# Order of the first pairs' work in a sliding-window attention with a feed-forward layer: mask products, sums and zero fills moved between queues

## The chip, the cores and the metric

The kernel runs on one core of a Trainium2 chip. Its time is the device time of one execution in microseconds (us); several executions are timed and the median is taken. A core has five engines that run side by side, each with its own queue of instructions in order: TensorE (PE, matrix products into PSUM), VectorE (DVE), ScalarE (ACT), GpSimd (POOL) and SyncE (SP, which here only issues transfers). They wait for each other by semaphores. [...]

## The reference

```python
# q, k, v: (8 batches, 8 heads, 576 tokens, 64)
scores = q @ k.T / sqrt(64)              # per batch and head
scores = where(|i - j| <= 32, scores, -1e9)
attn = softmax(scores)
x = attn @ v                             # joined over heads: (4608, 512)
h = x @ w_in                             # (512, 2048)
g = maximum(0.01 * h, h)
out = g @ w_out                          # (2048, 512)
```

## The kernel before

Matrix products are in bf16, sums in fp32 PSUM. Heads go in pairs, so a batch has four pairs (128 rows of head dimension), and batches 0 and 1 (`BY_DMA = 2`) are done in halves of 288 tokens: attention step i of these is batch i // 8, half (i // 4) % 2, pair i % 4 (`where`). From step 16 (`OLD`) on, batches 2 to 7 are done in another form, in groups of four blocks of 64 tokens (`score_blocks`, `product_blocks`), with two buffers `sets[0]` and `sets[1]` used in turn.

For batch 0 one attention step is spread over the engines like this:

- `load_qk` (SP) brings the queries and keys of a pair in fp32; `load_cast_v` (POOL queue) brings the values of one head at a time as bf16 onto the diagonal blocks of `vbd`, whose other blocks have to be zero. Two such loads belong to a pair.
- `cast_qk` casts queries (`qb`) and keys (`kb`) to bf16; the engine of each can be chosen, and POOL is the default. L270 is its line for VectorE and POOL, L268 for ScalarE.
- `transposes` (a generator: each `next` does the queries or the keys of one pair) transposes on TensorE (L308); ScalarE copies the result out (L316 queries, L322 keys).
- `score(i)`: ten small matmuls (L409), the exponential on ScalarE (`e`, L421), and the product with the mask (`prob`, L423) on POOL, for step 0 on VectorE. In the changed file these two are two lines further up.
- `sums(i)`: two matmuls with a matrix of ones (L447) and VectorE's reciprocal (L452).
- `product(i)`: five matmuls of values and probabilities (L463); `scaled(i)`: VectorE multiplies by the reciprocal (L477) and writes `xT`, the input of the feed-forward layer.

`s` and `x`, the PSUM tiles of sums and products, have one buffer each, so a sum waits until the reciprocal before it is done, and a product until the scaling before it is done. The score tile `ps` has one for these steps too. The reciprocals `r` have three.

The order within each engine is that of the program text (`manual_schedule`), with no planner for this part. Feed-forward work for a half of 288 tokens is 16 hidden tiles (`h_tile`, L501 and L512), each of four chunks, one for each pair. The first four tiles of the first half go chunk by chunk (`h_first`), so that the chunk of a pair can start when that pair is scaled. `warm_up` (L602) and `keep_busy` (L610) are matmuls whose results nobody uses. `load_w_in` and `load_w_out` bring the weights in four parts each, on POOL's queue (L661, L665).

Batch 1 is prepared meanwhile. `kbd[1]` (keys on diagonal blocks) and `vbd[1]` (values) lie in `sets[1]` and each have four blocks of 128 x 1152, one for each pair, which are filled with zeros: six of the eight on POOL in the loop of the hidden tiles (L750), two on VectorE (L771). `clear_half(i, p, a, eng)` fills the unused half of the queries' place `qz[i]` for two pairs, which batches from 2 on read; for `qz[1]` two of the four calls come at the start on ScalarE (L221) and two in `second_pair` on VectorE (L226). `second_pair(p)` transposes batch 1's pairs and starts casts and loads. In the later part `step()` does one attention step, started from a plan of the feed-forward matmuls (`spend`).

Of the kernel before, what the change touches and what calls it, by code (L numbers as in the profile page):

```python
# [10 lines left out]
BF16 = mybir.dt.bfloat16  # L11
AF = mybir.ActivationFunctionType
# [4 lines left out]
def kernel(  # L17
# [15 lines left out]
    nc = tc.nc  # L33
# [8 lines left out]
    NB = S // 64  # L42
    HALF = S // 2
# [6 lines left out]
    const = ctx.enter_context(tc.tile_pool(name="const", bufs=1))  # L50
# [94 lines left out]

    ident_f = sets[1].bitcast(FP32)[:, N_SET // 2 - 320:N_SET // 2 - 192]
    make_identity(nc, ident_f)
    for p in range(2):
        nc.vector.memset(vbd[0][:, p], 0.0)
    ident = const.tile([128, 128], BF16)  # L150
# [3 lines left out]
    nc.vector.memset(ones_bd, 0.0)  # L154
    nc.vector.memset(ones_bd[0:64, 0:64], 1.0)
    nc.vector.memset(ones_bd[64:128, 64:128], 1.0)


    zero = const.tile([128, 1], BF16)
    nc.vector.memset(zero, 0.0)  # L160

    mask = [const.tile([128, 2, 2, EVEN], BF16, name=f"mask{i}") for i in range(2)]
    nc.vector.memset(mask[0][:, 1, :, 0:16], 0.0)
# [52 lines left out]
    def clear_half(i, p, a, eng):  # L216

        r = slice(64 * (1 - a), 64 * (1 - a) + 64)
        to = qz[i][r, p:p + 2, :, a].rearrange("p n g s -> p (n g) s")
        if eng is nc.scalar:  # L220
            eng.activation(  # L221
                out=to, in_=zero[r].to_broadcast([64, 2 * S]).rearrange("p (g s) -> p g s", s=192),
                func=AF.Copy,
            )
        else:
            eng.memset(to, 0.0)  # L226
# [35 lines left out]
    def cast_qk(b, p, q_eng=nc.gpsimd, k_eng=nc.gpsimd):  # L262
        for eng, src, dst in ((q_eng, qf, qb), (k_eng, kf, kb)):
            if eng is None:
                continue
            to, tok = dst[:, p], src[b, p].rearrange("p a (c d) -> p c a d", d=D)
            if eng is nc.scalar:
                eng.activation(out=to, in_=tok, func=AF.Copy)  # L268
            else:
                eng.tensor_copy(out=to, in_=tok)  # L270
# [127 lines left out]
    def score(i, masked_by=nc.gpsimd):  # L398
        if i >= OLD:
            return score_blocks(i)  # L400
        b, hf, p = where(i)
        by_c = qT[b][:, p].rearrange("p (c i) -> p c i", c=2)
        if b == 0:

            for a, n_, m in ((0, 0, 0), (1, 1, 0), (0, 0, 1), (1, 1, 1), (0, 0, 2),
                             (0, 1, 0), (1, 0, 0), (0, 1, 1), (1, 0, 1), (1, 0, 2)):
                blk, i0, n = WIN[hf][n_][m]
                r = slice(64 * a, 64 * a + 64)
                nc.tensor.matmul(  # L409
                    ps_v[r, n_, :, i0:i0 + n], first_keys[p][r, 64 * blk:64 * blk + 64],  # L410
                    by_c[r, :, hf * EVEN + i0:hf * EVEN + i0 + n], start=True, stop=True,
                )
        else:
            for n_, blocks in enumerate(WIN[hf]):
                for blk, i0, n in blocks:
                    nc.tensor.matmul(
                        ps_v[:, n_, :, i0:i0 + n], kbd[b % 2][:, p, blk],
                        by_c[:, :, hf * EVEN + i0:hf * EVEN + i0 + n], start=True, stop=True,
                    )
        e = attn.tile([128, 2 * HALF], BF16, name="e")  # L420
        nc.scalar.activation(out=e, in_=ps[:, P0:P0 + 2 * HALF], func=AF.Exp, scale=scale)  # L421
        pr = prob[:, i % NPROB]
        masked_by.tensor_mul(  # L423
            pr.rearrange("p n c i -> p (n c i)"), e, mask[hf].rearrange("p n c i -> p (n c i)"),
        )
        probs[i] = [pr, None, None]
# [123 lines left out]
    def h_first(g):  # L550

        hs = [mmps.tile([128, 512], FP32, name="mm", tag="mm") for _ in range(4)]
        yield hs[0]
        for c in range(DMC):
            for f in range(4):
                h_mms(g, f, hs[f], (c,))
            if c == DMC - 1:
                for f in range(4):
                    h_out(g, f, hs[f])
            yield  # L560
# [45 lines left out]
    def keep_busy(t, lo, n):  # L606


        for _ in range(n):
            nc.tensor.matmul(  # L610
                t[:, lo:lo + 224], ones_bd, mask[0].rearrange("p n c i -> p (n c i)")[:, 0:224], start=False, stop=False,
                skip_group_check=True,
            )
# [16 lines left out]
    def step():  # L630
        i = state["done"]
        if JOINED - 1 <= i < OLD - 1:
            join(i + 1)
        if i < NC - 2:
            score(i + 2)
        weighted(i)
        place_keys()
        place_queries()
        for b, p in qk_due.get(i, ()):
            cast_qk(b, p)  # L640
            transpose_dma(b, p)
        if i == OLD - 2:
            for a in range(2):
                clear_half(0, 2, a, nc.gpsimd)
        if i == OLD + NPAIR:
            clear_k(1)
            set_ones(1, 0, nc.gpsimd)
            set_ones(1, 2, nc.gpsimd)
        for b, p in v_due.get(i, ()):
            cast_vw(b, p)  # L650
        for part in v_next.get(i, ()):
            load_v_pairs(*part)
        for b, p in qk_next.get(i, ()):
            load_qk(b, p)
        state["done"] += 1
# [4 lines left out]
    def load_w_in(f0, f1):  # L660
        nc.gpsimd.dma_start(out=w_in_bf[:, :, f0:f1], in_=w_in_r[:, :, f0:f1])  # L661

    def load_w_out(i):
        c = slice(4 * i, 4 * i + 4)
        nc.gpsimd.dma_start(out=w_out_bf[:, c, :], in_=w_out_r[:, c, :])  # L665

    first = transposes(0)

    for a in range(2):
        clear_half(1, 0, a, nc.scalar)  # L670
    cast_qk(0, 0, nc.vector, nc.vector)
    make_mask(0)
    load_cast_v(0, 0)
# [8 lines left out]
    next(first)  # L682
    next(first)
    load_cast_v(0, 3)
    load_w_in(0, 512)
    load_w_in(512, 1024)
    cast_qk(0, 2, nc.vector, nc.vector)
    sums(0)
    score(1)
    next(first)  # L690
    warm_up(2)
    next(first)
    cast_qk(0, 3, nc.scalar)
    warm_up(4)
    score(2)
    load_w_in(1024, 1536)
# [11 lines left out]
    keep_busy(ps, 0, 3)  # L708
    score(4)
    load_w_out(0)  # L710
    h0 = h_first(0)
    h = next(h0)
    product(2)
    scaled(2)
    keep_busy(h, HALF, 5)
    sums(3)
    next(h0)
    score(5)
    next(h0)
    for p in range(NPAIR):  # L720
        load_qk(1, p, nc.gpsimd if p == 0 else None)
    load_w_out(1)
    product(3)
    next(h0)
    scaled(3)
    sums(4)
    next(h0)
# [15 lines left out]
    for f in range(4, FFC):  # L743
        h_tile(0, f)
        if f in (4, 8, 12):
            second_half()
        if f == 4:
            load_w_out(3)
        if f % 2 == 1:
            nc.gpsimd.memset((kbd if f < 12 else vbd)[1][:, (f - 4) // 2 % 4], 0.0)  # L750
    second = transposes(1)
    def second_pair(p):
        next(second)
        next(second)
        place_keys()
        if p + 2 < NPAIR:
            cast_qk(1, p + 2, nc.vector, nc.gpsimd if p == 0 else None)
            clear_half(1, 2, p, nc.vector)
            if p == 0:
                load_cast_v(1, 1, (1,))  # L760
                load_cast_v(1, 2)
# [132 lines left out]
```

## Time and profile before

| | us |
|---|---|
| median of 3 timed runs | 315.7 |
| lowest, highest | 315.51, 316.58 |
| the profiled execution, its own time | 315.8 |
| its span, first to last instruction | 314.1 |

| engine | busy us | share of the span |
|---|---|---|
| TensorE | 300.7 | 96% |
| VectorE | 228.3 | 73% |
| POOL | 204.7 | 65% |
| ScalarE | 202.2 | 64% |

Times in the profile count from the span's start. In a timeline each row has the start, the duration, the engine, the line, the operation, its output and input with partitions x elements, and the count of instructions that were merged; in brackets stands the time that the engine was idle before it and what ended that. A merged row's duration runs from the first start to the last end. Matmuls overlap, so a row can end after the next has begun.

### The profile page before, as it was taken

Reading aid. Unit: us, or ns where it says so; the run is one execution under the profiler, and the core shown is the slowest. Engines: PE = TensorE matmul, PEld = TensorE weight load, DVE = VectorE, ACT = ScalarE, POOL = GpSimd, SP = SyncE. Lnnn points to the kernel's source line nnn. Section 1 sums busy time; section 2 is a strip of 40 time slices with the busy share of each in tenths; the row PEclk is TensorE's granted clock in tenths of the full one; section 3 lists DMA queues with packets and bytes.
Section 4 is the critical chain, followed back from the end, with each engine's and each line's share of the span. In section 5 each row is a group of like instructions: output and inputs, shape, how many; then the busy total and the mean of one; then the engine's idle time right before and its main releaser. Section 6 shows DMA issues by size and latency. Waiting matters only on the chain.

```text
span 314.1 us, 6755 instructions
## 1 busy us (share of the span) xinstructions
PE 300.7 (96%) x2541; PEld 195.7 (62%) x2541; DVE 228.3 (73%) x299; ACT 202.2 (64%) x419; POOL 204.7 (65%) x257
## 2 busy tenths in 40 slices
PE   1699999999999999999999999999999999999996
PEld 1566875576765858585858585858555555444643
DVE  7568988989669887889799776898679866753000
ACT  6635695375774858686858686767679548842731
POOL 8677999977799989498859357578947622110000
PEclk9999999999999999999999999999999999999999
DMA  7999999999999899979998997697970011001002
GB/s 192 195 183 183 260 232 107 243 182 179 191 231 190 138 262 180 221 151 244 205 169 172 247 221 130 155 217 157 195 139 2 13 69 56 0 35 67 33 26 77
DMA packets 122017, 48.29 MB, mean 154 GB/s; under 512 B 96256, under 2 KB 117504, under 8 KB 121984
## 3 DMA queue, kind: packets, MB, share of 16 engines
q1 hardware_dynamic: 108288, 42.48, 68.1%
q0 software_dynamic: 13696, 5.38, 14.5%
q8 instruction: 20, 0.33, 0.4%
q14 instruction: 13, 0.11, 0.1%
HBM read 36.70 MB, written 9.44 MB: 147 GB/s over the span
## 4 chain that ended last, share of the span: by engine, by line
PE 77%; POOL 11%; DMA 4%; DVE 3%; issue 2%; ACT 2%; SPq 0%; POOLq 0%; ACTq 0%; DVEq 0%
PE mm L574 34%; PE mm L501 33%; PE ps L361 3%; DVE r L452 2%; POOL set L750 2%; PE x L379 2%; PE s L379 2%; POOL kb L270 2%; POOL prob L368 2%; DMA set<-kb 1%; DMA kf<-in_k_dram 1%; POOL prob L423 1%; POOL qb L270 1%; POOL set L141 1%; PE s L447 1%
## 5 line engine op out<-in xcount | busy, mean ns | idle before, releaser
L501 PE MATMUL mm<-xT,w_in_bf 128*128 128x256 bf16 (+3 forms) x960 | 133.8, 294 | 0.0
L574 PE MATMUL mm<-w_out_bf,gT 128*128 128x512 bf16 (+2 forms) x560 | 124.6, 373 | 0.0
L388 DVE RECIPROCAL r<-r 128x256 f32<-128x256 f32 (+1 forms) x56 | 95.0, 1696 | 36.5 <-ACT r L387 36.1
L501 PEld LDWEIGHTS <-w_in_bf 128*128 128x128 bf16 x960 | 91.6, 98 | 30.2
L368 POOL TENSOR_TENSOR prob<-e,band 128x512 bf16<-128x512 bf16 (+1 forms) x56 | 62.6, 1117 | 54.8 <-ACT e L366 53.3
L574 PEld LDWEIGHTS <-gT 128*128 128x128 bf16 x560 | 52.1, 98 | 54.0
L512 ACT ACTIVATE gT<-mm 128x288 bf16<-128x288 f32 (+2 forms) x112 | 50.0, 478 | 12.1 <-PE mm L501 9.2
L366 ACT ACTIVATE e<-ps 128x512 bf16<-128x512 f32 (+1 forms) x56 | 32.4, 579 | 27.7 <-PE ps L361 24.1
L579 ACT ACTIVATE o_sb<-mm 128x512 f32<-128x512 f32 (+2 forms) x35 | 20.5, 585 | 39.3 <-PE mm L574 35.9
L535 ACT ACTIVATE gT<-mm 128x512 bf16<-128x512 f32 x64 | 35.7, 596 | 5.6 <-PE mm L501 4.2
L452 DVE RECIPROCAL r<-s 128x288 f32<-128x288 f32 x16 | 31.2, 1951 | 6.7 <-PE s L447 5.3
L392 DVE TENSOR_TENSOR xT<-s,r 64x256 bf16<-64x256 f32 (+1 forms) x56 | 24.3, 434 | 3.6 <-PE ps L361 0.5
L392 DVE TENSOR_TENSOR xT<-x,r 64x256 bf16<-64x256 f32 (+1 forms) x56 | 24.3, 435 | 3.3
L270 POOL CAST kb<-kf 96x768 bf16<-96x768 f32 x29 | 24.3, 838 | 1.4 <-DMA kf<-in_k_dram 0.9
L296 DVE COPY set<-kT 64x576 bf16<-64x576 bf16 x48 | 21.4, 446 | 2.7 <-DMA kT<-qb 1.8
L423 POOL TENSOR_TENSOR prob<-e,mask 128x576 bf16<-128x576 bf16 x15 | 19.2, 1278 | 5.7 <-ACT e L421 5.5
L361 PEld LDWEIGHTS <-set 128*128 128x128 bf16 x216 | 16.8, 98 | 9.7 <-DMA set<-kb 0.4
L361 PE MATMUL ps<-set 128*128 128x128 bf16 x216 | 21.4, 219 | 0.2 <-DMA set<-kb 0.2
L275 POOL CAST set<-vbuf 128x640 bf16<-128x640 f32 x24 | 17.2, 716 | 6.1 <-DMA vbuf<-in_v_dram 6.1
L270 POOL CAST qb<-qf 96x768 bf16<-96x768 f32 x24 | 19.7, 822 | 0.8 <-DMA qf<-in_q_dram 0.8
L379 PEld LDWEIGHTS <-set 128*128 128x128 bf16 x432 | 18.0, 98 | 0.5
L421 ACT ACTIVATE e<-ps 128x576 bf16<-128x576 f32 x16 | 10.5, 654 | 11.0 <-PE ps L409 7.6
(86 smaller groups left out, 249.7 us busy)
## 6 DMA issues: line engine op xcount, KB each, us to landing
qf<-in_q_dram SPq DMA_DIRECT2D x32, 288.0 KB, 5.9
kf<-in_k_dram SPq DMA_DIRECT2D x32, 288.0 KB, 6.3
out_dram<-o_sb SPq DMA_DIRECT2D x35, 256.0 KB, 2.8
vbuf<-in_v_dram SPq DMA_DIRECT2D x15, 256.0 KB, 4.9
w_in_bf<-in_moe_w_in_dram POOLq DMA_DIRECT2D x4, 512.0 KB, 7.3
w_out_bf<-in_moe_w_out_dram POOLq DMA_DIRECT2D x4, 512.0 KB, 11.3
vbuf<-in_v_dram SPq DMA_DIRECT2D x10, 192.0 KB, 4.6
set<-in_v_dram POOLq DMA_DIRECT2D x16, 72.0 KB, 5.9
```

Of the source, the lines that this page charges most:

```text
L270: eng.tensor_copy(out=to, in_=tok)
L361: nc.tensor.matmul(sc[:, :, w], kz[b % 2][:, p, 64 * m:64 * m + 128], tok[:, :, :, at:at + 32], start=True, stop=True,)
L366: nc.scalar.activation(out=e[:, 0:n], in_=ps[:, lo:lo + n], func=AF.Exp, scale=scale)
L368: nc.gpsimd.tensor_mul(pr, e[:, 0:n], band.rearrange("p w c i -> p (w c i)")[:, 0:n])
L379: nc.tensor.matmul(x[:, a, w], vw[b % 2][:, p, m, a:a + 2].rearrange("p n d -> p (n d)"), pr[:, a, w], start=True, stop=True,)
L388: nc.vector.reciprocal(r[:, 0:n], r[:, 0:n])
L392: nc.vector.tensor_mul(xT[rows, p, t0:t0 + n].rearrange("p (w i c) -> p w c i", i=32, c=2), x[rows, a].rearrange("p (w c i) -> p w c i", c ...
L452: nc.vector.reciprocal(r, s)
L501: nc.tensor.matmul(h[:, 0:n], w_in_bf[:, c, ts(f, 128)], xT[:, c, t0:t0 + n], start=(c == 0), stop=(c == DMC - 1),)
L512: nc.scalar.activation(out=to, in_=h, func=AF.Prelu, alpha=0.01)
L535: nc.scalar.activation(out=gT[:, f - 1:f + 1, t0:t0 + 256], in_=hh.rearrange("p (f t) -> p f t", f=2), func=AF.Prelu, alpha=0.01,)
L574: nc.tensor.matmul(o[:, lo:hi], gT[:, f, t0:t0 + 128], w_out_bf[:, f, lo:hi], start=(f == 0), stop=(f == FFC - 1),)
```

## The change

- The first mask product that POOL does (step 1) is put ahead of the first two parts of w_in in POOL's queue. To that end the calls of `load_w_in(0, 512)` and `load_w_in(512, 1024)` stand behind `score(1)`.
- The fourth pair's key cast of batch 0, `cast_qk(0, 3, ...)`, goes from POOL to VectorE, where it stands between the first and the second reciprocal.
- `sums(3)` stands ahead of `product(2)` and `scaled(2)`, so VectorE's fourth reciprocal is ahead of the third scaling. The five `keep_busy` matmuls there become three, ahead of `sums(3)`. The third chunk of `h_first` goes ahead of `product(3)`.
- Zero fills of batch 1's blocks: three blocks of `kbd[1]` on ScalarE at the start, in the place of two `clear_half` calls; the fourth on POOL ahead of the first mask product; two blocks of `vbd[1]` on POOL, behind the first and second part of w_out. The six fills in the loop of hidden tiles go.
- The four `clear_half` calls for `qz[1]` go to steps 16 to 19, on VectorE.
- `zero`, a column of zeros that ScalarE's fills read, is written by VectorE ahead of its other fills.

```diff
     make_identity(nc, ident_f)
+    zero = const.tile([128, 1], BF16)
+    nc.vector.memset(zero, 0.0)
     for p in range(2):
         nc.vector.memset(vbd[0][:, p], 0.0)
...
-    zero = const.tile([128, 1], BF16)
-    nc.vector.memset(zero, 0.0)
...
             for a in range(2):
                 clear_half(0, 2, a, nc.gpsimd)
+        if OLD <= i < OLD + 4:
+            clear_half(1, 2 * (i % 2), (i - OLD) // 2, nc.vector)
...
     first = transposes(0)
 
-    for a in range(2):
-        clear_half(1, 0, a, nc.scalar)
+    for p in range(3):
+        nc.scalar.activation(
+            out=kbd[1][:, p].rearrange("p n j -> p (n j)"),
+            in_=zero.to_broadcast([128, NB * 128]), func=AF.Copy,
+        )
...
     load_cast_v(0, 3)
-    load_w_in(0, 512)
-    load_w_in(512, 1024)
+    nc.gpsimd.memset(kbd[1][:, 3], 0.0)
     cast_qk(0, 2, nc.vector, nc.vector)
     sums(0)
     score(1)
+    load_w_in(0, 512)
+    load_w_in(512, 1024)
     next(first)
     warm_up(2)
     next(first)
-    cast_qk(0, 3, nc.scalar)
+    cast_qk(0, 3, nc.scalar, nc.vector)
     warm_up(4)
...
     keep_busy(ps, 0, 3)
     score(4)
     load_w_out(0)
+    nc.gpsimd.memset(vbd[1][:, 0], 0.0)
     h0 = h_first(0)
     h = next(h0)
+    keep_busy(h, HALF, 3)
+    sums(3)
     product(2)
     scaled(2)
-    keep_busy(h, HALF, 5)
-    sums(3)
     next(h0)
     score(5)
     next(h0)
     for p in range(NPAIR):
         load_qk(1, p, nc.gpsimd if p == 0 else None)
     load_w_out(1)
+    nc.gpsimd.memset(vbd[1][:, 1], 0.0)
+    next(h0)
     product(3)
-    next(h0)
     scaled(3)
     sums(4)
...
-        if f % 2 == 1:
-            nc.gpsimd.memset((kbd if f < 12 else vbd)[1][:, (f - 4) // 2 % 4], 0.0)
...
             cast_qk(1, p + 2, nc.vector, nc.gpsimd if p == 0 else None)
-            clear_half(1, 2, p, nc.vector)
```

## The prediction

> **What bounds the kernel now.** I read the page first, then TensorE's waits, then the timeline of each engine over the first 30 us.
>
> ```profile
> PE 300.7 (96%) x2541; PEld 195.7 (62%) x2541; DVE 228.3 (73%) x299; ACT 202.2 (64%) x419; POOL 204.7 (65%) x257
> ```
>
> The view of the cores gives the span and the mean granted clock:
>
> ```profile
> core 0: 314.1 us, clock 1.000
> ```
>
> TensorE is busy in 96% of the span, so 13.4 us of the 314.1 are idle, and TensorE sets the end: what another engine does faster counts only where TensorE stands still for it, or where TensorE itself is given less to do. The profiled execution took 315.8 us, 1.7 more than its span; the three timed runs have a median of 315.7 (315.51 to 316.58). I sum against 315.8 and take 0.1 off at the end. A measurement of this kernel can tell about 0.3%, 0.95 us, from no change.
>
> ```profile
> PE s L447 <- POOL prob L423: 2.2, 1, 2.2
> PE ps L409 <- ACT kT L322: 1.1, 2, 0.7
> PE s L447 <- DVE r L452: 0.8, 3, 0.3
> ```
>
> The columns are the total, the times and the longest. After the start the first of these rows is the one long wait, and it is a single one; all other kinds together are small, 0.7 at the longest. The timeline of TensorE shows it (start, duration, idle time before it and its releaser in brackets):
>
> ```profile
> 12.97 0.66 PE L409 MATMUL ps<-set,kT 64*64 64x96 bf16 x10 [0.31 <-ACT kT L322]
> 15.81 0.64 PE L447 MATMUL s<-prob,ones_bd 128*128 128x288 bf16 x2 [2.18 <-POOL prob L423]
> ```
>
> The column sums of the second pair (L447, `sums(1)`) come 2.18 us after TensorE had finished `score(2)` at 13.63. They wait for the second mask product, and POOL's timeline says why that is late:
>
> ```profile
> 4.09 6.34 POOL L141 DMA_DIRECT2D set<-in_v_dram  x8
> 12.89 1.53 POOL L661 DMA_DIRECT2D w_in_bf<-in_moe_w_in_dram  x2 [2.46 <-DMA set<-in_v_dram]
> 14.49 1.27 POOL L423 TENSOR_TENSOR prob<-e,mask 128x576 bf16<-128x576 bf16 x1
> ```
>
> POOL issues eight loads of V until 10.43, is idle 2.46 us until a slot of its DMA queue is free, issues two loads of w_in until 14.42, and only then takes the product. Its input was there long before:
>
> ```profile
> 10.99 0.65 ACT L421 ACTIVATE e<-ps 128x576 bf16<-128x576 f32 x1 [0.77 <-PE ps L409]
> ```
>
> The exponential ends at 11.64. So the product stands some 2.8 us behind its input, in a queue that did nothing for most of that time.
>
> **Part 1: the product ahead of the weights.** In the changed program POOL's order is V loads, one zero fill, product 1, the two w_in loads, product 2; the third pair's key cast goes from POOL's queue to VectorE. A zero fill of one block costs 6.05 / 6 = 1.01 us:
>
> ```profile
> 32.80 6.05 POOL L750 MEMSET set<- 128x1152 bf16 x6
> ```
>
> POOL: 10.43 + 1.01 = 11.44, so the exponential's end at 11.64 decides, and product 1 runs from 11.7 to 13.0 in place of 14.49 to 15.76. The w_in loads start at 13.0 in place of 12.89, 0.1 us later, and end at 14.5; product 2 follows, to 15.8. TensorE reaches `sums(1)` when `score(2)` is through, 13.6 in place of 15.81: the wait goes as a whole, 2.2 us.
>
> What is late next is VectorE's reciprocal of these sums:
>
> ```profile
> 10.85 1.96 DVE L452 RECIPROCAL r<-s 128x288 f32<-128x288 f32 x1
> 16.49 1.96 DVE L452 RECIPROCAL r<-s 128x288 f32<-128x288 f32 x1 [3.69 <-PE s L447]
> ```
>
> It starts 0.68 us after its matmuls (16.49 against 15.81), so at 14.3, if VectorE is free. After the first reciprocal, done at 12.81, VectorE now has the key cast. The groups of the first 62 us have three such casts on VectorE, all made while POOL issued V loads:
>
> ```profile
> L270 DVE CAST kb<-kf 96x768 bf16<-96x768 f32 x3 | 2.5, 834 | 0.7 <-DMA kf<-in_k_dram 0.6
> ```
>
> At their mean of 0.83 us it ends at 13.64, before 14.3, and costs nothing. But a cast can be slower:
>
> ```profile
> 45.21 2.18 DVE L270 CAST qb<-qf 96x768 bf16<-96x768 f32 x1
> ```
>
> A query cast of the same shape took 2.18 us there, while POOL was in a cast and then in DMA issues (its 44.78 row, below, and what follows it). From 12.81 POOL is just so placed: in a product, then in two DMA issues. At 2.18 us the cast ends at 15.0, and the reciprocal starts 0.7 us later than 14.3. Bounds 0 and 0.7; I take 0.1: the three key casts are the nearest, and they had DMA issues beside them too. [...]
>
> From there to `score(4)` the order of work is unchanged and each step hangs on the one before (sums, reciprocal, scaling, next sums; product 2 at 15.8 is in time for sums that wait for the reciprocal's end at 16.3). So these steps come 2.2 us earlier, or 2.1 with the 0.1 above.
>
> **Part 2: the fourth pair's sums ahead of the third's values.**
>
> ```profile
> 20.57 0.72 PE L610 MATMUL ps<-mask,ones_bd 128*128 128x224 bf16 x3 [0.25 <-ACT e L421]
> 21.21 0.66 PE L409 MATMUL ps<-set,kT 64*64 64x64 bf16 x10
> 21.81 0.64 PE L463 MATMUL x<-prob,set 128*128 128x96 bf16 x5
> 22.23 1.14 PE L610 MATMUL mm<-mask,ones_bd 128*128 128x224 bf16 x5
> 23.17 0.69 PE L447 MATMUL s<-prob,ones_bd 128*128 128x288 bf16 x2
> 23.65 0.98 PE L501 MATMUL mm<-xT,w_in_bf 128*128 128x288 bf16 x4
> 24.56 0.43 PE L409 MATMUL ps<-set,kT 64*64 64x64 bf16 x10
> ```
>
> Before: `score(4)` at 21.21, the third pair's product, five filler matmuls (L610), `sums(3)` at 23.17, the first chunk of the first hidden tiles. After: `score(4)` at 19.0 to 19.6, three fillers at (23.17 - 22.23) / 5 = 0.19 each to 20.2, `sums(3)` to 20.7 (its mask product is done by 19.7), the product to 21.1, then the first chunk. The two fillers dropped save 0.4 us of TensorE. VectorE:
>
> ```profile
> 22.48 0.46 DVE L477 TENSOR_TENSOR xT<-x,r 128x288 bf16<-128x288 f32 x1 [1.01 <-PE x L463]
> 23.89 1.96 DVE L452 RECIPROCAL r<-s 128x288 f32<-128x288 f32 x1 [0.96 <-PE s L447]
> 25.95 0.46 DVE L477 TENSOR_TENSOR xT<-x,r 128x288 bf16<-128x288 f32 x1
> 26.60 1.96 DVE L452 RECIPROCAL r<-s 128x288 f32<-128x288 f32 x1 [0.19 <-PE s L447]
> ```
>
> The fourth reciprocal starts at 20.9 and ends at 22.85 (before 23.89 to 25.85), 3.0 us earlier; the third pair's scaling, now behind it, ends at 23.3, 0.4 later than before (22.94). The third chunk needs that scaling. TensorE's first chunk, `score(5)` and second chunk take 0.98, 0.6 and 0.98 at the pace of 23.65, so from 21.1 to 23.6, and 23.3 is covered, just. Then third chunk to 24.5, fourth product to 24.9, its scaling 0.46 to 25.4, fourth chunk at 25.4, where it was at 26.47:
>
> ```profile
> 26.47 0.65 PE L501 MATMUL mm<-xT,w_in_bf 128*128 128x288 bf16 x4
> ```
>
> That is a gain of 1.1 us at this point. The fifth reciprocal, on which the next sums wait, starts when the scaling is done, at 25.4 against 26.60: a gain of 1.2.
>
> It hangs on TensorE's pace. The 23.65 row has four matmuls of 288 columns in 0.98, the 26.47 row in 0.65; the scores go from 0.66 to 0.43 for ten. The pace doubled near 24.4, though the granted clock above is 1.000 all through, so I read the pace from durations alone. If that comes at the same moment as before, the gain is 1.2. If it comes 2.2 us earlier with the work, the first two chunks and the score take about half, TensorE waits for the third scaling until 23.3, the third chunk at half its time ends at 23.8, the product at 24.0, the fourth scaling at 24.5, and the fifth reciprocal starts 2.1 earlier than before. I take the middle, 1.65. [...]
>
> **Part 3: the fills.** ScalarE:
>
> ```profile
> 2.99 0.41 ACT L248 ACTIVATE ps<-zero 128x288 f32<-128x288 bf16 x1 [0.89 <-DVE zero L160]
> 3.43 2.33 ACT L221 ACTIVATE set<-zero 64x1152 bf16<-64x1152 bf16 x2
> ```
>
> and, further on,
>
> ```profile
> 7.01 0.65 ACT L322 ACTIVATE kT<-tp 128x576 bf16<-128x576 bf16 x1 [0.72 <-PE tp L308]
> ```
>
> Its first fill waited 0.89 us for `zero`, which VectorE now writes first. From 2.1: 0.41, then three fills at 2.33 / 2 = 1.16 end at 6.0, against 3.43 + 2.33 = 5.76 before. The first query copy stands behind them and ends at 6.65 if it takes the 0.65 of the key copy in the 7.01 row, which waits for TensorE until 7.01 with 0.72 us idle: nothing is lost; without that cover it would be 0.25. POOL's fills behind w_out stand ahead of products 5 and 6:
>
> ```profile
> 25.83 1.27 POOL L423 TENSOR_TENSOR prob<-e,mask 128x576 bf16<-128x576 bf16 x1 [1.08 <-ACT e L421]
> ```
>
> and
>
> ```profile
> 28.73 1.27 POOL L423 TENSOR_TENSOR prob<-e,mask 128x576 bf16<-128x576 bf16 x1 [0.83 <-ACT e L421]
> ```
>
> Each has 1.08 and 0.83 us of idle time ahead for 1.01: nothing for the first, 0.2 us for the second, whose sums stand behind several hidden tiles. The six fills at 32.80 go; they stood on the chain that the page follows, but TensorE has no wait there, so this gives nothing by itself. VectorE's four half fills move from batch 1's set-up to steps 16 to 19:
>
> ```profile
> 47.46 0.54 DVE L226 MEMSET set<- 64x576 uint32 x1
> ```
>
> VectorE's waits from 76 to 112 us have first
>
> ```profile
> DVE r L388 <- ACT r L387: 5.2, 6, 1.4
> ```
>
> Four would be 2.2 us; it waits 5.2 us for ScalarE in six pieces there, some 0.9 each beside 0.54: nothing, 0.3 where a piece is short.
>
> **The loads.** w_in's first chunk is issued 0.1 us later:
>
> ```profile
> DMA to landing us min/median/max: 5.7/7.3/8.5
> ```
>
> With 8.5 us, the longest, it lands at 21.5, with 5.7 at 18.7; it is wanted at 21.1. I take 0, since this load lands at 5.7 in the trace, and 0.4 as the other end. Batch 1's loads are started by POOL behind product 5, 2.2 us earlier; its keys of the third pair are the tightest:
>
> ```profile
> 30.07 0.40 SPq L80 DMA_DIRECT2D kf<-in_k_dram  x1
> ```
>
> The landing times of this issue (the last figure) and the one ahead of it, then the cast and its reader:
>
> ```profile
> DMA to landing us min/median/max: 12.0/12.6/13.1
> ```
>
> POOL:
>
> ```profile
> 44.78 0.84 POOL L270 CAST kb<-kf 96x768 bf16<-96x768 f32 x1
> ```
>
> TensorE:
>
> ```profile
> 45.68 0.43 PE L308 MATMUL tp<-ident,kb 96*128 96x96 bf16 x6
> ```
>
> Issue at 30.07 plus 13.1 is 43.2. The cast (0.84) could end at 44.05, and TensorE wants it at 45.68 minus the gain. With a gain of 1.6 that is just met even if the load lands no earlier.
>
> **Sum.** 1.65 (parts 1 and 2, the middle of 1.2 and 2.1) less 0.1 for the cast and 0 for fills and loads: 1.55. 315.8 - 1.55 = 314.25; as a median, 0.1 lower, 314.2 rounded up. The forecast covers gains of 1.1 to 1.9.
>
> **Rivals.**
> - *The pace comes with the work.* Gain 2.1: 315.7 - 2.1 = 313.6; the loads of batch 1 then hold TensorE for at most 0.5 of it. For it: after the change TensorE's work from 16 us on has fewer holes. Against it: fewer fillers. Chance 0.2.
> - *VectorE's cast is held by POOL.* The 2.18 us of the 45.21 row: 0.7 off 1.2 or 1.65 leaves 0.5 to 0.95, so 314.75 to 315.2. For it: POOL's queue has no hole from 11.7 to 15.8. Against it: the casts beside V issues. Chance 0.2.
> - *Nothing is left of it.* A later stage gives it back (loads of batch 1, or VectorE at steps 16 to 19 pushing scores): 315.4 to 315.8. Against it: TensorE's waits for VectorE are 0.3 at the longest (the third row of its waits), so there is room before a later step becomes a wait. Chance 0.1.
> - *TensorE's double pace comes later: slower.* In the trace the pace doubled 3.8 us after the last hole (0.25 ahead of the 20.57 row). If the waits for the third and fourth scaling tear a hole at 25.0, before the pace has changed, it changes at 28.8, and 4.4 us of work run at half pace, 2.2 more; less the gain of 1.2 that is 1.0 slower, 316.7. It decides at whether 23.3, the scaling, comes before 23.6, the end of the second chunk; there are 0.3 us. Chance 0.08.
>
> **Chances and range.** The forecast has 0.42. Faster by over 0.3% is below 314.75: the forecast, the first rival and a quarter of the second make 0.67. Within: the rest of the second and the third, 0.25; slower 0.08. The range runs from 313.3, the first rival with one wait of 0.3 for VectorE gone too, to 315.4, the far end of the second and 0.2 for a short piece of the fills; outside are the slower case and most of the third.
>
> **What would show it.** Right: product 1 on POOL at 11.7 with both w_in issues behind; no wait of `sums(1)` over 0.3 us; the fourth reciprocal near 20.9; fourth chunk between 24.4 and 25.4; no new wait of TensorE over 0.5 us after 30 us. The cast on VectorE after 12.8 shows 0.8 or over 2. Wrong: a hole ahead of the third chunk, scores of 0.66 us per ten after 25 us, or TensorE waiting for batch 1's keys near 44 us.

## The result, and the profile after

| | median us | lowest, highest | ratio to before, 95% interval |
|---|---|---|---|
| before (6 runs beside it) | 315.52 | 314.55, 316.58 | |
| changed (6 runs) | 312.69 | 312.47, 313.14 | 0.9913 [0.9892, 0.9934] |
| changed, six more (`e10_again`, further down) | 313.38 | 313.18, 313.57 | 0.9900 [0.9882, 0.9917] |

The change made the kernel faster, by 2.7 us in the first comparison (0.0087 of 315.5) and 3.2 in the second (0.0100 of 316.5). The forecast was 1.5, its range 313.3 to 315.4: the sign was right, the size too small. The profiled execution took 313.14 us. Its view of the cores, then its page (busy time; the chain that ended last):

```profile
core 0: 311.4 us, clock 1.000
```

```profile
PE 299.7 (96%) x2539; PEld 194.8 (63%) x2539; DVE 224.3 (72%) x302; ACT 203.3 (65%) x420; POOL 200.6 (64%) x253
...
PE 92%; DMA 3%; DVE 2%; issue 1%; SPq 1%; ACT 0%; ACTq 0%
```

The span is 2.7 us shorter. TensorE has 1.0 less busy time (two matmuls fewer, and a little more work at the double pace) and 1.7 less idle time (11.7 in place of 13.4). POOL's timeline of the changed kernel has the new order (start, duration, then the idle time before the row and its releaser):

```profile
10.36 1.33 POOL L688 MEMSET set<- 128x1152 bf16 x1
12.18 1.27 POOL L421 TENSOR_TENSOR prob<-e,mask 128x576 bf16<-128x576 bf16 x1 [0.48 <-ACT e L419]
13.68 1.58 POOL L661 DMA_DIRECT2D w_in_bf<-in_moe_w_in_dram  x2 [0.22 <-issue]
15.26 1.29 POOL L421 TENSOR_TENSOR prob<-e,mask 128x576 bf16<-128x576 bf16 x1
```

The product waits for its own input now, the exponential, and the weights stand behind it. TensorE's timeline:

```profile
13.57 0.66 PE L407 MATMUL ps<-set,kT 64*64 64x96 bf16 x10 [0.31 <-ACT kT L320]
14.16 0.66 PE L445 MATMUL s<-prob,ones_bd 128*128 128x288 bf16 x2
...
20.72 0.63 PE L445 MATMUL s<-prob,ones_bd 128*128 128x288 bf16 x2
21.19 0.40 PE L461 MATMUL x<-prob,set 128*128 128x96 bf16 x5
...
23.71 0.65 PE L499 MATMUL mm<-xT,w_in_bf 128*128 128x288 bf16 x4 [0.68 <-DVE xT L475]
...
25.15 0.65 PE L499 MATMUL mm<-xT,w_in_bf 128*128 128x288 bf16 x4 [0.30 <-DVE xT L475]
...
27.02 0.42 PE L445 MATMUL s<-prob,ones_bd 128*128 128x288 bf16 x2
...
78.10 0.40 PE L377 MATMUL x<-prob,set 128*128 128x64 bf16 x8
...
103.86 0.40 PE L377 MATMUL s<-prob,set 128*128 128x64 bf16 x8
...
297.96 10.56 PE L572 MATMUL mm<-w_out_bf,gT 128*128 128x512 bf16 x64
```

The first row is `score(2)`. The 14.16 row has no bracket: the wait of 2.18 us ahead of `sums(1)` is gone. Two new holes stand at 23.71 and 25.15, ahead of the third and the fourth chunk. The last four rows, held against the same rows of the kernel before, tell where the time was won. In what follows the lead of a kernel is the time by which a matmul starts earlier in it than in the profile of before:

```profile
28.61 0.42 PE L447 MATMUL s<-prob,ones_bd 128*128 128x288 bf16 x2 [0.30 <-DVE r L452]
...
80.31 0.40 PE L379 MATMUL x<-prob,set 128*128 128x64 bf16 x8
...
106.26 0.34 PE L361 MATMUL ps<-set 128*128 128x128 bf16 x3 [0.20 <-DMA set<-kb]
106.44 0.40 PE L379 MATMUL s<-prob,set 128*128 128x64 bf16 x8
...
300.60 10.56 PE L574 MATMUL mm<-w_out_bf,gT 128*128 128x512 bf16 x64
```

The lead is 1.59 us at `sums(5)` (28.61 - 27.02), 2.21 at 80 us, 2.58 at 106 and 2.64 at the last group of matmuls. So 1.59 came in the first 28 us, where the sum had 1.55, 0.62 between 28 and 80 us, where the sum had nothing, and 0.37 near 104 us, where the wait of 0.20 in the 106.26 row is gone. From 106 us on nothing more came.

That 1.59 is so near 1.55 is in part luck. `score(2)` started 0.60 us later in this execution than in the one of before (13.57 against 12.97), since VectorE had waited 1.56 us for a load of queries ahead of a cast at 7.46. In all fifteen profiles this start lies between 12.30 and 13.65, and `e10_again`, the same program as the changed kernel, has the 12.30. From `score(2)` on the changed kernel won 2.19 us by `sums(5)` in the first profile and 1.87 in the second.

### The profile page after: what moved, and what is told of

The parts are those of the page before. It is cut to its first block, busy times and chain, and to the rows that moved or that the text cites. A ratio compares the mean times of both kernels' runs of the same rounds, so it can differ in the third digit from the quotient of the medians.

```text
span 311.4 us, 6749 instructions
## 1 busy us (share of the span) xinstructions
PE 299.7 (96%) x2539; PEld 194.8 (63%) x2539; DVE 224.3 (72%) x302; ACT 203.3 (65%) x420; POOL 200.6 (64%) x253
## 4 chain that ended last, share of the span: by engine, by line
PE 92%; DMA 3%; DVE 2%; issue 1%; SPq 1%; ACT 0%; ACTq 0%
PE mm L499 40%; PE mm L572 38%; PE ps L359 4%; DMA kf<-in_k_dram 3%; PE mm L588 2%; PE s L377 2%; PE x L377 2%; DVE r L450 1%; PE s L445 1%; PE x L461 1%; SPq L80 1%; PE tp L306 1%; PE ps L407 1%; PE ps L414 1%; DVE kb L268 1%
## 5 line engine op out<-in xcount | busy, mean ns | idle before, releaser
L364 ACT ACTIVATE e<-ps 128x512 bf16<-128x512 f32 (+1 forms) x56 | 32.4, 579 | 27.6 <-PE ps L359 25.5
L268 POOL CAST kb<-kf 96x768 bf16<-96x768 f32 x28 | 23.5, 839 | 5.1 <-DMA kf<-in_k_dram 5.1
L294 DVE COPY set<-kT 64x576 bf16<-64x576 bf16 x48 | 21.4, 446 | 0.9
```

The source lines that it names most:

```text
L364: nc.scalar.activation(out=e[:, 0:n], in_=ps[:, lo:lo + n], func=AF.Exp, scale=scale)
```

## The experiments

Each was run in six or twelve timed executions beside the kernel before; ratios are to it. Line numbers in rows of `e5_half`, `e7_nobusy`, `e8_poolcast`, `e9_refill`, `e10_again` and `e12_vfirst` are two lower, like those of the changed kernel.

**First question: which part of the change brings it?** Four kernels, each with some of the parts.

`e1_order` is the kernel before with part 1 alone (POOL's order and the key cast on VectorE):

```diff
-    load_w_in(0, 512)
-    load_w_in(512, 1024)
     cast_qk(0, 2, nc.vector, nc.vector)
     sums(0)
     score(1)
+    load_w_in(0, 512)
+    load_w_in(512, 1024)
...
-    cast_qk(0, 3, nc.scalar)
+    cast_qk(0, 3, nc.scalar, nc.vector)
```

> The kernel before with the order of POOL's queue alone changed: product 1 ahead of the first two w_in loads, and the fourth pair's key cast on VectorE (sums, fillers and zero fills as before). The sum's theory (the wait of 2.2 us goes, TensorE's pace comes partly with it): 1.2 to 2.1 us faster than before, sums(1) without its 2.18 us wait. Rival A (the two orders give only together what they give, since the fourth reciprocal stays behind five fillers): under 1.0 us faster. Rival B (most of the gain comes from the zero fills that leave POOL's queue): at most 1.0 us faster.

`e2_sums` is the kernel before with part 2 alone:

```diff
+    keep_busy(h, HALF, 3)
+    sums(3)
     product(2)
     scaled(2)
-    keep_busy(h, HALF, 5)
-    sums(3)
...
-    product(3)
     next(h0)
+    product(3)
```

> The kernel before with the second part alone: the fourth pair's sums ahead of the third's product, three fillers in place of five, the third chunk ahead of the fourth product. The sum's theory: the fourth reciprocal starts about 0.8 us earlier, the third scaling later; 0.2 to 0.6 us faster. Rival A (the orders work only together): within 0.2 us of before. Slower by up to 0.5 us if the third chunk now waits for its scaling at the full pace.

`e3_fills` is the kernel before with all lines on zero fills of the change (`zero` first, three blocks on ScalarE, three on POOL at the start, `clear_half` at steps 16 to 19) and no other:

```diff
-        if f % 2 == 1:
-            nc.gpsimd.memset((kbd if f < 12 else vbd)[1][:, (f - 4) // 2 % 4], 0.0)
...
-            clear_half(1, 2, p, nc.vector)
...
```

> The kernel before with the zero fills alone changed (zero first; three fills on ScalarE; one on POOL ahead of the w_in loads; two behind w_out; none in the loop; half fills at steps 16 to 19). My prediction put this at nothing: within 0.2 us of before. The theory from the two traces: about 1.0 us faster, in three places: TensorE's transposes of batch 1's third keys near 45.7 us come 0.2 us earlier, the reciprocals near 56 us 0.4, and the scores that waited for transposed keys near 106 us 0.4; up to 40 us its timeline is that of before within 0.2 us.

`e4_nofills` is the changed kernel with these lines as before, so parts 1 and 2 together:

```diff
+        if f % 2 == 1:
+            nc.gpsimd.memset((kbd if f < 12 else vbd)[1][:, (f - 4) // 2 % 4], 0.0)
...
+            clear_half(1, 2, p, nc.vector)
...
```

> The changed kernel without the zero fills' part: both orders, all fills as before. The sum's theory with my prediction's zero for the fills: the whole gain, 2.5 to 2.9 us faster than before. The theory from the traces (fills are worth about 1.0): 1.6 to 1.9 us faster, all of it reached by 40 us, with TensorE's small waits near 45, 56 and 106 us as before or longer.

| kernel | median us | before us | ratio, 95% interval |
|---|---|---|---|
| `e1_order`, part 1 | 313.54 | 315.73 | 0.9925 [0.9899, 0.9950] |
| `e2_sums`, part 2 | 315.94 | 315.73 | 1.0011 [0.9989, 1.0033] |
| `e3_fills`, part 3 | 315.07 | 315.73 | 0.9981 [0.9965, 0.9998] |
| `e4_nofills`, parts 1 and 2 | 313.53 | 315.73 | 0.9935 [0.9913, 0.9957] |

Part 1 brings 2.4 us (1.6 to 3.2) by itself, with part 2 it is 2.1 (1.4 to 2.7), and part 2 alone is no change. So the early gain is part 1, POOL's order with the key cast, and the sums' order adds nothing that these runs can tell. The fills bring 0.6 (0.1 to 1.1). 2.1 and 0.6 make the 2.7 of the whole; but part 1 alone, at 2.4, is not told apart from the whole either, and why is seen below.

The profile of `e3_fills` is 0.79 us behind before at `sums(5)`, where it was expected to be level: its `sums(1)` waited 2.74 us in place of 2.18, and its matmuls doubled their pace later. From there it won 0.63 by 80 us. Where this 0.6 lies in the changed kernel is seen between 40 and 57 us, while batch 1 is set up; it comes in two steps. The first is the transposes of keys that stood at 45.68 in the kernel before, right behind POOL's key cast (44.78 to 45.62): they waited for it. POOL and TensorE of the changed kernel at that place:

```profile
41.33 1.03 POOL L268 CAST kb<-kf 96x768 bf16<-96x768 f32 x1
```

```profile
43.86 0.42 PE L306 MATMUL tp<-ident,kb 96*128 96x96 bf16 x6
```

The cast is done at 42.36, 1.5 us before it is wanted, since POOL no longer comes to it through 6.05 us of fills. The lead grows by 0.24 here (45.68 - 43.86 = 1.82, from 1.59). The second step is the sums that waited for VectorE's reciprocal; the kernel before, then the changed one:

```profile
56.30 0.42 PE L447 MATMUL s<-prob,ones_bd 128*128 128x288 bf16 x2 [0.23 <-DVE r L452]
```

```profile
54.10 0.42 PE L445 MATMUL s<-prob,ones_bd 128*128 128x288 bf16 x2
```

The lead is 2.20 behind it, 0.37 more than at the sums before. VectorE, without a pause over 0.18 us from 45.21 to the reciprocal that ended the wait, had been late there since the fourth query cast of batch 1, 2.18 us (45.21), and a half fill behind it (47.46). In the changed kernel that fill is gone and the cast is short:

```profile
43.56 0.59 DVE L268 CAST qb<-qf 96x768 bf16<-96x768 f32 x1
```

**Second question: which fills, and by which of the two steps?** `e9_refill` puts the six POOL fills back on top of the changed kernel, and `e10_again` is the changed kernel once more beside it:

```diff
+        if f % 2 == 1:
+            nc.gpsimd.memset((kbd if f < 12 else vbd)[1][:, (f - 4) // 2 % 4], 0.0)
```

> The changed kernel with the six fills of the loop of hidden tiles put back on POOL on top of those it has (the blocks are filled a second time, ahead of batch 1's keys). Theory (the six fills on POOL between 30 and 37 us hold VectorE's query casts and put off POOL's key casts, and this is what moving them away is worth): 0.4 to 0.7 us of the gain are lost, 2.0 to 2.4 us faster than before; VectorE's first query casts take over 1 us each, and TensorE's row of the sums near 54 us waits again. Rival (the fills' place is worth nothing, the rest of the change gives it all): as the changed kernel, 2.6 us or more.

> The changed kernel once more, on the same chip and in the same rounds as its variants: 2.5 to 3.0 us faster than before, as first measured. In its profile a first sum (sums(1)) at 13.4 to 13.7 where the first loads land as in the other runs, not at 14.16, and the sums behind the fourth scaling correspondingly earlier than 27.0.

`e5_half` puts two of the four half fills back on VectorE in `second_pair`:

```diff
-        if OLD <= i < OLD + 4:
-            clear_half(1, 2 * (i % 2), (i - OLD) // 2, nc.vector)
+        if i in (OLD, OLD + 2):
+            clear_half(1, 0, (i - OLD) // 2, nc.vector)
...
+            clear_half(1, 2, p, nc.vector)
```

> The changed kernel with two of the half fills back in batch 1's set-up on VectorE, where they were (near 42 and 46 us), the other two at steps 16 and 18. Theory (what the fills' part is worth, some 0.6 us, comes from POOL's six fills that no longer stand ahead of batch 1's casts and so no longer hold VectorE's casts): as the changed kernel, 2.5 to 3.0 us faster than before; VectorE's four query casts between 35 and 46 us take 0.55 to 0.9 each. Rival (VectorE itself was too full near 44 to 56 us, and the two half fills of 0.54 are what counts): 2.0 to 2.3 us faster, with a wait of TensorE for a reciprocal near 54 us.

`e9_refill` took 314.02 us (0.9922 [0.9900, 0.9944]), `e10_again` 313.38, `e5_half` 313.12 (0.9915 [0.9886, 0.9944]). By the medians the six fills cost 0.64 against `e10_again` and the two half fills nothing against the changed kernel, but the intervals overlap, and `e9_refill` lost time at another place too (fourth question); the steps are told apart in the timelines. POOL and TensorE of `e9_refill`:

```profile
30.91 6.07 POOL L756 MEMSET set<- 128x1152 bf16 x6
...
42.63 0.84 POOL L268 CAST kb<-kf 96x768 bf16<-96x768 f32 x1
```

```profile
43.53 0.43 PE L306 MATMUL tp<-ident,kb 96*128 96x96 bf16 x6
```

The key cast is late again, the transposes start 0.06 us behind its end (43.47), and the lead does not grow here (2.16 at `sums(5)`, 2.15 here): the first step is the six fills' doing. It is theirs by a narrow margin, though. `e1_order` keeps them where they were and has no such wait: POOL's key cast ends at 43.92 there, and the transposes follow at 44.10 right behind those of the queries. The fills also hold VectorE, as was expected: its first two query casts in `e9_refill`, then in the changed kernel,

```profile
34.86 3.63 DVE L268 CAST qb<-qf 96x768 bf16<-96x768 f32 x2
```

```profile
35.43 1.10 DVE L268 CAST qb<-qf 96x768 bf16<-96x768 f32 x2
```

but no wait of TensorE follows from that. For the second step, VectorE in `e9_refill`, in `e5_half` and in `e1_order`, at the fourth query cast:

```profile
43.09 2.15 DVE L268 CAST qb<-qf 96x768 bf16<-96x768 f32 x1
```

```profile
43.70 1.55 DVE L268 CAST qb<-qf 96x768 bf16<-96x768 f32 x1 [0.43 <-DMA qf<-in_q_dram]
45.31 0.54 DVE L224 MEMSET set<- 64x576 uint32 x1
```

```profile
43.94 0.56 DVE L270 CAST qb<-qf 96x768 bf16<-96x768 f32 x1
44.56 0.54 DVE L226 MEMSET set<- 64x576 uint32 x1
```

| kernel | fourth query cast, us | half fill behind it | wait of the sums near 53 to 56 us |
|---|---|---|---|
| before | 2.18 | yes | 0.23 |
| `e2_sums` | 2.16 | yes | 0.23 |
| `e4_nofills` | 1.75 | yes | 0.22 |
| `e5_half` | 1.55 | yes | 0.16 |
| `e1_order` | 0.56 | yes | none |
| `e9_refill` | 2.15 | no | none |
| `e6_oldsums` | 1.56 | no | none |
| changed, `e3_fills` | 0.59, 0.56 | no | none |

The wait stands only where a long cast and a half fill come together; either alone fits into VectorE's room. So the half fills' move takes the second step even with a long cast (`e9_refill`, `e6_oldsums`), and a short cast does as well, which is why `e1_order`, with all its old fills, has the whole 0.6 too (1.34 to 1.97 in the table of leads below). POOL works beside the long casts: in the kernel before it issues V loads from 45.54 to 47.74,

```profile
45.54 2.20 POOL L141 DMA_DIRECT2D set<-in_v_dram  x3
```

and the cast that begins at 45.21 ends at 47.39. The first two casts took 3.63 us beside the fills (`e9_refill`) and 1.10 without them. But work of POOL beside it does not tell the short fourth casts from the long ones, since POOL issues V loads beside the short ones too: in `e1_order` these issues stood from 43.82 to 46.27,

```profile
43.82 2.45 POOL L141 DMA_DIRECT2D set<-in_v_dram  x3
```

the cast began at 43.94, 0.12 us behind the first of them, and it took 0.56; in `e4_nofills` it began 0.10 us behind and took 1.75. In the changed kernel it began 1.25 us behind and took 0.59, in `e5_half` 1.10 behind and 1.55. In the three kernels with over 2 us it began while POOL's key cast still ran. What decides the length stays open.

**Third question: the key cast, the order of the sums, the fillers.** Three kernels from the changed one. `e8_poolcast` puts the key cast back on POOL, behind the weights; `e6_oldsums` the old order of the sums with five fillers; `e7_nobusy` takes the six fillers around `score(4)` out:

```diff
-    cast_qk(0, 3, nc.scalar, nc.vector)
+    cast_qk(0, 3, nc.scalar)
```

> The changed kernel with the fourth pair's key cast back on POOL, behind product 1 and the two w_in loads and ahead of product 2. Theory (VectorE has room for the cast between its first two reciprocals, and POOL has none): product 2 and with it sums(2) come 0.4 to 0.8 us later, 0.3 to 0.8 us of the gain are lost (2.0 to 2.5 us faster than before). Rival (VectorE's cast is held by POOL and costs as much): as the changed kernel or better, 2.8 us or more.

```diff
-    keep_busy(h, HALF, 3)
-    sums(3)
     product(2)
     scaled(2)
+    keep_busy(h, HALF, 5)
+    sums(3)
...
```

> The changed kernel without the sums' part: the order of POOL's queue and the zero fills changed, the fourth pair's sums behind the third's product and five fillers as before. Theory (the sums' part is worth nothing, since the third scaling then waits behind the fourth reciprocal): 2.6 to 3.0 us faster than before, like the changed kernel, with no wait of TensorE for a scaling. Rival (my prediction's step: the fourth reciprocal 0.8 us earlier is part of the gain): 2.0 to 2.3 us faster.

```diff
-    keep_busy(ps, 0, 3)
     score(4)
...
-    keep_busy(h, HALF, 3)
```

> The changed kernel without the six fillers around score(4). If TensorE's pace hangs on how densely it is filled between 17 and 22 us (the slower rival): its matmuls double their pace 2 us later or more, scores of 0.66 us for ten still after 25 us, and 0.5 to 2 us are lost against the changed kernel (1.0 to 2.3 faster than before). If the pace does not hang on them: 0 to 0.5 us better than the changed kernel, since six matmuls of 0.19 go, up to 3.2 faster than before.

They took 313.40 (0.9921 [0.9898, 0.9944]), 313.27 (0.9925 [0.9899, 0.9951]) and 313.36 (0.9920 [0.9895, 0.9944]), beside 315.76 for the kernel before: the interval of each holds the changed kernel's ratios, 0.9913 and 0.9900, so none can be told from it. With the cast on POOL TensorE waits once more, in the timeline of `e8_poolcast`

```profile
15.65 0.66 PE L306 MATMUL tp<-ident,kb 96*128 96x96 bf16 x6 [0.60 <-POOL kb L268]
```

and the third pair's sums behind it stand 3.88 us behind `score(2)`, against 3.31 and 3.60 in the two profiles of the changed kernel and at most 3.66 in any with the cast on VectorE. So its move is worth some 0.2 to 0.6 us at that place; at `sums(5)` the lead of `e8_poolcast` is 1.75, and in its time nothing of it can be told. Without the fillers the double pace comes late. `e7_nobusy`, TensorE:

```profile
21.77 0.66 PE L407 MATMUL ps<-set,kT 64*64 64x64 bf16 x10
...
24.71 0.69 PE L445 MATMUL s<-prob,ones_bd 128*128 128x288 bf16 x2
...
26.16 0.43 PE L407 MATMUL ps<-set,kT 64*64 64x64 bf16 x10
```

The change of pace lies between 24.71 and 26.16, and the lead at `sums(5)` is 1.16, the smallest of all kernels with part 1. That is the direction of the forecast's slower rival, but the lead only shrank, by 0.4 us against the changed kernel's first profile and 1.4 against its second; it did not turn round.

`e11_three` tells the number of fillers from the order of the sums: three fillers as in the changed kernel, the sums behind the scaling and the chunks as before.

```diff
     keep_busy(h, HALF, 3)
-    sums(3)
     product(2)
     scaled(2)
+    sums(3)
...
```

> Both orders of the changed kernel's POOL queue and its fills, but the third pair's product and scaling ahead of the fourth pair's sums, with three fillers ahead of both. Theory (the changed kernel loses about 1 us in two waits for scalings, at 23.7 and 25.2, which this order has not, and gains nothing from the earlier reciprocal): up to 40 us TensorE is 0.3 to 1.0 us ahead of the changed kernel; the whole 2.8 to 3.4 us faster than before, unless the transposed keys of batch 3 near 104 us hold it, when it is the same as the changed kernel. Rival (the earlier reciprocal counts): 2.2 to 2.6 us faster.

It took 313.39 (0.9899 [0.9880, 0.9917]) beside `e10_again`'s 313.38. In the time of the whole neither the order of the sums nor the two fillers are worth anything that can be told. Up to `sums(5)` the old order does rather better: counted from `score(2)`, `e6_oldsums` won 2.76 us and `e11_three` 2.42, the changed kernel 2.19 and 1.87. What becomes of that is the next question.

**Fourth question: what holds the kernels that lead most?** The leads over the profile of before, in us, each the start of the same matmuls in both traces (one profile of each kernel). The first column is the start itself, which differs between executions of one program (-0.60 and 0.67 in the first two rows); the gain of the first pairs' order is the second column less the first:

| kernel | `score(2)` | `sums(5)` | 80 us | 106 us | last group |
|---|---|---|---|---|---|
| changed | -0.60 | 1.59 | 2.21 | 2.58 | 2.64 |
| `e10_again` | 0.67 | 2.54 | 3.16 | 2.18 | 2.24 |
| `e1_order` | -0.48 | 1.34 | 1.97 | 2.18 | 2.24 |
| `e2_sums` | 0.03 | -0.12 | -0.14 | 0.14 | 0.20 |
| `e3_fills` | 0.19 | -0.79 | -0.16 | 0.22 | 0.28 |
| `e4_nofills` | 0.12 | 1.77 | 1.76 | 2.14 | 2.20 |
| `e5_half` | -0.29 | 1.85 | 2.16 | 2.12 | 1.84 |
| `e6_oldsums` | -0.08 | 2.68 | 3.32 | 3.12 | 2.65 |
| `e7_nobusy` | -0.01 | 1.16 | 1.77 | 2.15 | 2.21 |
| `e8_poolcast` | -0.03 | 1.75 | 2.36 | 2.74 | 2.80 |
| `e9_refill` | 0.06 | 2.16 | 2.50 | 0.59 | 0.66 |
| `e11_three` | 0.07 | 2.49 | 3.12 | 2.30 | 2.36 |
| `e12_vfirst` | -0.68 | 1.43 | 2.05 | 1.52 | 1.58 |
| `e13_three_vfirst` | 0.13 | 2.22 | 2.85 | 2.67 | 2.29 |

The 0.37 that the changed kernel won near 104 us is not shown to be the change's: `e2_sums`, which is no faster than before, won 0.28 there, and `e4_nofills`, with the old fills, 0.38. The wait of 0.20 in the profile of before may belong to that one execution.

Who leads by 2.5 us or more at 80 us gives some back near 104 us. TensorE and VectorE in `e10_again`, and TensorE in `e9_refill`:

```profile
104.09 0.33 PE L359 MATMUL ps<-set 128*128 128x128 bf16 x3 [1.19 <-DVE set L294]
```

```profile
103.13 0.91 DVE L294 COPY set<-kT 64x576 bf16<-64x576 bf16 x2 [2.50 <-DMA kT<-qb]
```

```profile
105.68 0.33 PE L359 MATMUL ps<-set 128*128 128x128 bf16 x3 [1.66 <-DVE set L294]
```

The scores of a later batch wait for queries and keys that are transposed by DMA. These transposes are issued on SP's queue, with five loads of V between the first pair's and the second's, so `e12_vfirst` puts the V loads ahead of both, on the changed kernel, and `e13_three_vfirst` does the same on `e11_three`:

```diff
+        if i == OLD:
+            for b, p in v_due.pop(i, ()):
+                cast_vw(b, p)
+            for part in v_next.pop(i, ()):
+                load_v_pairs(*part)
...
```

> The changed kernel with one more move: in step 16 the last V cast of batch 2 and batch 3's V loads go ahead of that step's transposes by DMA, so that the five V loads no longer stand between the first and the second pair's transposes in SP's queue. In the second profile of the changed kernel (its third run label) TensorE led the kernel before by 3.16 us at 80 us and by 2.2 at the end, and waited 1.19 us near 104 us for batch 3's keys. Theory (the V loads in SP's queue put off the second pair's transposes by some 4 us): no wait over 0.3 us there, the lead at 80 us is kept, 3.0 to 3.4 us faster than the kernel before. Rival (the transposes are held by the DMA engines or by POOL's casts, not by the queue's order): the wait stays, 2.3 to 2.8 us faster, as the changed kernel. A third outcome: the V cast ahead of the key casts on POOL delays them, and up to 1 us more is lost.

> The same move of the V loads on the version with three filler matmuls, the old place of the third pair's product and the old chunk order (which led by 3.12 us at 80 us and by 2.36 at the end, with a wait of 1.04 us near 104 us). Theory: the wait goes, 3.0 to 3.4 us faster than the kernel before. Rival: the wait stays, 2.3 to 2.8 us faster.

They took 313.48 (0.9897 [0.9864, 0.9929]) and 313.49 (0.9898 [0.9865, 0.9931]): as the changed kernel. TensorE's wait in `e12_vfirst` is 0.60, in `e13_three_vfirst` 0.39 (1.04 in `e11_three`). SP's timelines of `e10_again` and `e12_vfirst` say why the move did not bring the second pair forward:

```profile
92.95 4.14 SPq L106 DMA_DIRECT2D vbuf<-in_v_dram  x5
...
98.05 1.24 SPq L280 DMA_TRANSPOSE kT<-qb  x1
```

```profile
87.99 7.27 SPq L106 DMA_DIRECT2D vbuf<-in_v_dram  x5
...
98.79 1.23 SPq L280 DMA_TRANSPOSE kT<-qb  x1
```

The five loads took 7.27 us in place of 4.14, and the second pair's transposes were issued 0.74 us later, not 4 earlier. In `e10_again` the transpose that stood first took 4.09 us, in `e12_vfirst`, behind the loads, 1.39: in these two kernels whichever stands first carries some 3 us (2.7 and 3.1) that are not its own. So the theory that the loads, by standing between, put off the second pair falls. Whether the move helps a little is not told: `e13_three_vfirst` lost 0.18 us of its lead near 104 us where `e11_three` lost 0.82, but `e12_vfirst` lost 0.53 from a lead of only 2.05, where the changed kernel lost nothing from 2.21. The waits end between 103.1 and 106.3 us in the kernels that have them, and no run here tells whether the loads of queries and keys, the DMA engines or the casts ahead set that moment; it stays open.

## Why the prediction was wrong

By its own steps:

- *The wait of `sums(1)` goes as a whole.* Right. `e1_order` shows that this alone is most of the result. Product 1 ran at 12.18, not 11.7, because the exponential was later, and `sums(1)` at 14.16, not 13.6, because `score(2)` was; nothing of POOL's was in the way.
- *The key cast costs 0.1, bounds 0 and 0.7.* Right (it is the fourth pair's, which the working of part 1 calls the third's): 0.84 us, between the reciprocals, beside two issues of POOL, so the rival in which it is held did not happen. In the ten other kernels that have this cast on VectorE it took 0.49 to 1.30.

```profile
14.02 0.84 DVE L268 CAST kb<-kf 96x768 bf16<-96x768 f32 x1
14.86 1.96 DVE L450 RECIPROCAL r<-s 128x288 f32<-128x288 f32 x1
...
21.39 1.96 DVE L450 RECIPROCAL r<-s 128x288 f32<-128x288 f32 x1 [1.54 <-PE s L445]
23.26 0.40 DVE L475 TENSOR_TENSOR xT<-x,r 128x288 bf16<-128x288 f32 x1
...
25.01 1.95 DVE L450 RECIPROCAL r<-s 128x288 f32<-128x288 f32 x1
```

- *Parts 1 and 2 are worth 1.65, the middle of 1.2 and 2.1.* The bounds held, nearly: the fifth reciprocal came 1.59 us earlier in the changed kernel's profile (25.01 against 26.60), the leads at `sums(5)` of the kernels with part 1 are 1.16 to 2.68, and by the medians parts 1 and 2 are worth 2.1. The middle was low by some 0.4, though the interval of that 2.1 (1.4 to 2.7) holds it. In the first profile the pace had come with the work, the first rival's case, and its 2.19 from `score(2)` on is that rival's 2.1; the late start hid 0.60 of it. The reason given for part 2 fell: "23.3 is covered, just" was not. The scaling ended at 23.66 and TensorE stood still for 0.68 us, because both chunks and the score between them, from 21.4 on, already ran at the double pace; the sums ahead of the values gain nothing over the old order (`e6_oldsums`, `e11_three`).
- *The fills give nothing.* **This step failed.** "TensorE has no wait there, so this gives nothing by itself" looked only beside the six fills. Their price stood 7 us behind their end, at the key transposes of 45.68, which the forecast quoted as an allowance for a load and did not read as a wait for POOL's cast. For the half fills it reckoned only what they cost at the place they go to, 0 to 0.3, and not what they leave: VectorE's lateness and the 0.23 ahead of the sums at 56.30. Measured 0.24 and 0.37, 0.6 us together, in place of 0; `e3_fills`, the fills alone, took 0.6 less (0.1 to 1.1). Of the 1.2 us between the forecast's 1.55 and the measured 2.7 this is about one half; the size of parts 1 and 2, by the medians, is the other.
- *The range.* Its low end took the better pace and 0.3 more, 313.3, and had no term for the fills; with 0.6 it would have been 312.7. The first six runs lie below that end of 313.3, the six of `e10_again` at it.
- *Loads.* Right up to 100 us: in the changed kernel's trace no chunk and no transposes of TensorE wait for a DMA after the start. Near 104 us the lead meets transfers, as told; 0.37 of the lead there is a wait that the profile of before had and that of the changed kernel had not; no part of the sum stood for it, and `e2_sums` shows most of it without any gain in time.
- *The pace.* The forecast had it at the same moment as before or 2.2 us earlier with the work. The rows show neither as a rule. In the changed kernel the pace doubles between 20.72 and 21.19 (five products in 0.40). TensorE in `e10_again`, the same program with `sums(1)` 1.1 us earlier, and in `e4_nofills`:

```profile
13.07 0.64 PE L445 MATMUL s<-prob,ones_bd 128*128 128x288 bf16 x2
...
20.65 1.17 PE L499 MATMUL mm<-xT,w_in_bf 128*128 128x288 bf16 x4
21.75 0.44 PE L407 MATMUL ps<-set,kT 64*64 64x64 bf16 x10
```

```profile
22.29 0.66 PE L409 MATMUL ps<-set,kT 64*64 64x64 bf16 x10
```

The work is 1.1 us earlier and the double pace some 0.6 later (the chunk at 20.65 still takes 1.17), and in `e4_nofills` it comes after 22.29. What sets this moment no run here shows; the two moments that the forecast took, and the middle between their gains, 1.65, were its author's estimate.

## What to carry to other kernels

An instruction that waits in a queue that itself does nothing is the cheapest thing to move: the 2.18 us of one row came back nearly whole (1.82 us from `score(2)` to `sums(5)` in `e1_order`). Work that is moved is to be costed at both ends: what it costs where it goes, and who was late behind it where it leaves, even 7 or 8 us further on and on another engine. And a gain at the start has to pass every later stage that hangs on transfers; here the five kernels that led by 2.5 us or more at 80 us lost 0.2 to 1.9 us of it near 104 us. And one profile beside one other carries where the start fell in each: here `score(2)` lay up to 0.7 us either way.

## What the runs showed of the hardware

- A VectorE cast of 96x768 to bf16 took 0.55 us with POOL idle for most of it (two in 1.10, changed kernel at 35.43), 3.63 for two beside POOL's zero fills, and up to 2.18 beside POOL's key cast and issues of V. But the key cast beside two issues of weights took 0.84, and casts beside V's issues took 0.56 and 0.59, so an issue of POOL's beside it does not by itself make a cast long.
- The moment at which TensorE's matmuls double their pace (ten of 64 columns in 0.66 us, then in 0.43 to 0.44) varied by 4 us between kernels that start alike (21 to 25.5 us), while the mean granted clock was 0.999 or 1.000 for all. Between two executions of one program it moved by some 0.6 us, against the work.
- Moving five loads ahead of two transposes in one queue made the loads' issue 3.1 us longer (7.27 against 4.14), that of the first transpose 2.7 shorter (1.39 against 4.09), and won nothing: the queue's time was not the loads' own.
